# An mLSTM cell and a two-layer feed-forward on one core: the first product from chunk 1 on as three float32r products of 12-bit halves

## The chip, the cores and the metric

The kernel runs on one core of a Trainium2 chip. The metric is the device time of one execution in microseconds (us), the median of several runs. Engines are called TensorE (PE; its weight loads are PEld), VectorE (DVE), ScalarE (ACT), GpSimd (POOL) and SyncE (SP, which here only issues DMAs). SBUF is the on-chip memory with 128 partitions, PSUM holds the sums of TensorE in eight banks of 512 fp32 columns.

## The reference

Four batches, eight heads, 768 steps, head dimension 40. A recurrent attention (mLSTM) gives for each step a row of 320 = 8 x 40 values; the 3072 rows go through a feed-forward with a gelu of sigmoid form.

```python
for t in range(S):
    m_new = np.maximum(f_gate[:, :, t] + m, i_gate[:, :, t])
    f_stab = np.exp(f_gate[:, :, t] + m - m_new)
    i_stab = np.exp(i_gate[:, :, t] - m_new)
    C = f_stab * C + i_stab * outer(vt, kt)
    n = f_stab * n + i_stab * kt
    y[:, :, t] = sigmoid(o_gate) * (C @ qt) / np.maximum(abs(n @ qt), 1.0)
x = y as (3072, 320)
h = x @ w_in                                   # (3072, 2048)
g = h * (1.0 / (1.0 + np.exp(-1.702 * h)))
out = g @ w_out                                # (3072, 320)
```

All inputs are fp32 in value; the host hands them over as float64 bit pairs for `w_in` and `w_out`, which the kernel converts (lines 240 to 266).

## The kernel before

**Chunks.** The 768 steps are cut into six chunks w = 0 to 5 of 128 steps; a chunk has 4 x 128 = 512 tokens. The order of all work is written out by hand (`manual_schedule`): the loop over w at the end of the kernel issues, for each chunk, its first product `up`, then its second product `down`, and between the blocks of `down(w)` the attention of chunk w+1. Engines run their own instructions in the order in which they are issued, so a VectorE operation written behind another waits for it.

**First product.** `w_in` is held as 16 tiles of 128 output columns, two of its 320 rows' parts in `w_in_sb` (128 rows each) and the last 64 rows in `w_in_x`. Two tiles make a pair j, eight pairs make a chunk. Chunk 0 uses plain fp32 products (`up`, L626, L635). From chunk 1 on `up_fast` uses a scheme with seven products instead of eight for a 2 x 2 block product (Strassen's, in Winograd's form): half the tokens (256 columns) by sums of weight blocks. The weight sums are made once, in `input_sums` (L668 to L671, between blocks 11 and 13 of `down(0)`); the token sums in `token_sums` (L679 to L684) at the start of each chunk. Each pair is seven fp32 products of 256 columns (L724) and the products of the last 64 rows over 512 columns, two side by side on half the array's rows (L703). VectorE, ACT and POOL put the results together (L741, L763 to L765, L777, L778, L784, L786), and ACT applies gelu (L692) into `gs`.

**Second product.** `down_fast` is again a seven-product scheme, over two halves c of seven blocks each, so blocks 0 to 13 (L847, sums on VectorE L850, L852, L832). The blocks read `gs` and `sums`; block 10 is the last that reads the first four tiles of `gs`, block 11 the last that reads the first kind of `sums`, block 13 the last that reads the second. `store(1)` stands behind block 12 and `store(0)` behind block 13 (L856). `down(0)` is a plain product of 16 blocks (L793).

**Attention of the next chunk.** After each block the call list `attention(w + 1)` adds steps: gate columns (L367), weights (ACT L435, POOL L439), state products (`carry`, L602, L611, with `decay`, L579, and `scale`, L588), scores (L459, L462), values (L503, L511, L517 and on), then `seam_out` and `seam_in`, which send the result through DRAM, and `seam_turn` (VectorE, L572), which writes it transposed as `xT`, the input of the next first product. In the list the two halves of `seam_turn` stand behind blocks 10 and 11 (for chunk 1 behind blocks 12 and 14).

**Queues.** Nearly all DMAs are issued by SP in the written order. Ahead of block 13 SP issues `load_squares(w + 2)` (k and q of the chunk after next, L108), which `block_transposes` (L394) read during the next first product. During the first product SP issues the gate rows (`m_row`, `st_row`, `d_row`, L304 to L331), the o_gate load, the gate columns (`columns_in`, L350, L352), `spread` (L403) and the v and k loads (L120) of chunk w+1.

**Buffers.** Tiles with the same tag share buffers in turn: `gp` has eight of 4 KB per partition (`gs`), `sp` has four (`sums`), a new tile waits until the old one in its buffer is last read. `ps_m` is four PSUM banks, `ps_a` two pairs of banks.

Of the kernel before, what the change touches and what calls it, by code (L numbers as in the profile page):

```python
# [8 lines left out]
FP = mybir.dt.float32  # L9
U32 = mybir.dt.uint32  # L10
BF = mybir.dt.bfloat16
AF = mybir.ActivationFunctionType
OP = mybir.AluOpType
# [5 lines left out]
NEG = -1.0e30  # L19

# [6 lines left out]
def kernel(  # L27
# [33 lines left out]
    work = ctx.enter_context(tc.tile_pool(name="work", bufs=2))  # L61
    gp = ctx.enter_context(tc.tile_pool(name="gp", bufs=NH))
# [16 lines left out]
    s_in = const.tile([128, 3, NF // 2, 128], FP, name="s_in")  # L79
# [5 lines left out]
    w_in_sb = const.tile([128, 2, DFF], FP, name="w_in_sb")  # L85
    w_in_x = const.tile([128, NF // 2, 128], FP, name="w_in_x")
# [46 lines left out]
    def piece_in(c, n):  # L133
        return (w_in_sb[:, c, n * 512:(n + 1) * 512],
                [(slice(0, 128), slice(0, 512), w_in_bits[c:256:2, n * 1024:(n + 1) * 1024])])
# [21 lines left out]
    def fetch(n):  # L157
        if n < 3 or 10 <= n < 13:
            bits[n] = s_in[:, n % 10].rearrange("p j m -> p (j m)").bitcast(U32).rearrange("p (a two) -> p a two", two=2)
        elif n == 17:  # L160
            bits[n] = t_flat[:, at_bits:at_bits + 1024].bitcast(U32).rearrange("p (a two) -> p a two", two=2)
        else:
            bits[n] = (gp if 6 <= n < 10 else sp).tile([128, 512, 2], U32, tag="g", name="bits")
# [34 lines left out]
    ident = const.tile([128, 128], FP, name="ident")  # L198
# [155 lines left out]
    def columns_turn(w):  # L354
        c = cols[w] = gate.tile([L, 4 * BH], FP, name="cols")
# [3 lines left out]
    def columns(w):  # L359
        if w == 0:  # L360
            pt = banks("p_cols")[:, 0, :]
            T.transpose(pt[:, 0:3 * BH], stacked[w], full)
            c = cols[w] = gate.tile([L, 4 * BH], FP, name="cols")
# [157 lines left out]
    def x_of(w):  # L521
        if w not in xT:
            xT[w] = work.tile([128, 3, B, L], FP, tag="xT", bufs=1, name="xT")
        return xT[w]
# [43 lines left out]
    def seam_turn(w, c):  # L568
        for b in range(2):
            x = x_of(w)[:, :, 2 * c + b, :].rearrange("p c (r n) -> p n c r", n=4)  # L570
# [43 lines left out]
    def up(w, j, between):  # L614
# [5 lines left out]
        def full(j, first, cs=range(2)):  # L620
            for c in cs:
                for i in range(2):
                    f = 2 * j + i
                    for n in range(2):
                        t = slice(n * W // 2, (n + 1) * W // 2)
                        T.matmul(ph[j][i][:, t], w_in_sb[:, c, f * 128:(f + 1) * 128], x[:, c, t],  # L626
# [34 lines left out]
    half_w = W // 2  # L661
    temps, second = {}, {}

    def input_sums(js):

        a = lambda c, i: w_in_sb[:, c, :].rearrange("p (j two m) -> p j two m", two=2, m=128)[:, js, i, :]
        s1, s2, s4 = (s_in[:, n, js] for n in range(3))
        V.tensor_tensor(out=s1, in0=a(0, 1), in1=a(1, 1), op=OP.add)  # L668
        V.tensor_tensor(out=s2, in0=s1, in1=a(0, 0), op=OP.subtract)
        V.tensor_tensor(out=a(0, 1), in0=a(0, 0), in1=a(0, 1), op=OP.subtract)  # L670
        V.tensor_tensor(out=s4, in0=a(1, 0), in1=s2, op=OP.subtract)  # L671

    def token_sums(w):

        x = xT[w].rearrange("p c b t -> p c (b t)")
        b11, b12, b21, b22 = (x[:, c, n * half_w:(n + 1) * half_w] for c in range(2) for n in range(2))
        r = [work.tile([L, PH, D1], FP, tag="u", name="t_x").rearrange("p h d -> p (h d)") for _ in range(2)]
        x1, x2, x4 = r[0][:, 0:half_w], r[0][:, half_w:W], r[1][:, 0:half_w]
        V.tensor_tensor(out=x1, in0=b12, in1=b11, op=OP.subtract)  # L679
        V.tensor_tensor(out=x2, in0=b22, in1=x1, op=OP.subtract)  # L680
        V.tensor_tensor(out=b12, in0=b22, in1=b12, op=OP.subtract)
        V.tensor_tensor(out=x4, in0=b21, in1=x2, op=OP.subtract)
        rest = x[64:128, 2, :]
        V.tensor_tensor(out=rest[:, 0:half_w], in0=rest[:, 0:half_w], in1=rest[:, half_w:W], op=OP.subtract)  # L684
        temps[w] = {1: b11, 2: b21, 3: b22, 4: x4, 5: x1, 6: x2, 7: b12}
        second[w] = r[1][:, half_w:W]

    def gelu_fast(w, j, between=None):
        for i in (1, 0):
            if between and i == 0:  # L690
                between()
            A.activation(out=gs[w, j][:, i, :], in_=gs[w, j][:, i, :], func=AF.Gelu_apprx_sigmoid)  # L692

    row_banks = {}

    def row_product(w, j, start):

        n = 2 if w == NW - 2 or (w == NW - 3 and j < 2) else 1
        for h in range(n):
            t = slice(h * W // n, (h + 1) * W // n)  # L700
            for i, row in enumerate(row_banks[w, j]):
                r = slice(i * 64, i * 64 + 64)
                T.matmul(row[:, t], w_in_x[r, j, :], xT[w][r, 2].rearrange("p b t -> p (b t)")[:, t],  # L703
                         start=(start and h == 0), stop=(not start and h == n - 1))
# [4 lines left out]
    def up_fast(w, j):  # L709

        x = temps[w]
        k = j % 4
        left, right = slice(0, half_w), slice(half_w, W)
        f = lambda c, i: w_in_sb[:, c, (2 * j + i) * 128:(2 * j + i + 1) * 128]

        def product(n, out, start, stop):
            a = {1: lambda: f(0, 0), 2: lambda: f(1, 0), 3: lambda: s_in[:, 2, j], 4: lambda: f(1, 1),
# [16 lines left out]
        def copy_row():  # L739
            if apart:  # L740
                A.copy(out=g[:, 0, :], in_=row0)  # L741
# [296 lines left out]
```

## Time and profile before

| what | value |
|---|---|
| runs | 465.27 us median of three (463.86 to 467.92) |
| the profiled execution | 464.2 us, which is its span from the first to the last instruction |
| first product of chunks 1 to 5 | 112.65 to 144.50, 184.85 to 216.69, 256.09 to 287.94, 327.34 to 359.22, 398.46 to 430.30 us |
| granted TensorE clock | 1.000 of full speed in the mean |
| DMA | 52.87 MB, mean 114 GB/s over the span |

In the lines of the profile a group names the line of the kernel, the engine, the operation and output<-inputs, then the count, and after the bar the busy time and the mean of one. In the chain of work and in the timelines the columns are start, length and what, in us from the start of the span; a `q` behind an engine's name is its sequencer, which issues a DMA. An fp32 matmul shows as two instructions, each with its weight load.

### The profile page before, as it was taken

The numbers are of one execution on the slowest core, as the hardware profiler recorded it, in microseconds if no ns is written. First come the engines' busy times: TensorE is split into PE (matmuls) and PEld (weight loads), VectorE is DVE, ScalarE is ACT, GpSimd is POOL, SyncE is SP. The second block draws the span as 40 slices with busy tenths as digits, with TensorE's granted clock in tenths as the row PEclk, the third lists the DMA queues.
The fourth block names the chain that finished last, engine by engine and source line by source line (L and its number), as shares of the span: only waits on it lengthen the run. The fifth ranks groups of instructions, "written<-read, shape, count | busy, mean of one in ns | idle before, by whom it ended". The sixth has DMA issues, their size and how long they took to land.

```text
span 464.2 us, 12386 instructions
## 1 busy us (share of the span) xinstructions
PE 456.3 (98%) x5071; PEld 391.0 (84%) x5071; DVE 353.3 (76%) x738; ACT 186.4 (40%) x433; POOL 163.7 (35%) x154
## 2 busy tenths in 40 slices
PE   8999999899999999999999999999999999999996
PEld 6877887577779899779999779999888999787996
DVE  5788997989889975888786888787788766554622
ACT  5686779100556600455800354900264910164200
POOL 5101507200599600266800167610157710146200
PEclk9999999999999999999999999999999999999999
DMA  8999999018969025969224979315988505000000
GB/s 162 184 275 198 210 262 232 14 33 198 190 133 135 3 61 125 200 99 174 35 58 105 195 122 167 46 33 126 172 128 155 79 18 140 28 1 1 1 28 30
DMA packets 135561, 52.87 MB, mean 114 GB/s; under 512 B 101984, under 2 KB 131632, under 8 KB 135504
## 3 DMA queue, kind: packets, MB, share of 16 engines
q1 hardware_dynamic: 127136, 50.27, 55.6%
q10 hardware_dynamic: 8048, 1.66, 1.8%
q8 instruction: 40, 0.66, 0.7%
q0 software_dynamic: 320, 0.15, 0.2%
q14 instruction: 17, 0.14, 0.1%
HBM read 44.52 MB, written 7.54 MB: 112 GB/s over the span
## 4 chain that ended last, share of the span: by engine, by line
PE 79%; DMA 8%; DVE 7%; SPq 4%; issue 2%; ACT 0%; DVEq 0%
PE p_out L847 31%; PE p_h L724 22%; PE p_h L703 7%; PE p_out L793 3%; PE p_h L626 3%; PE p_o L503 2%; DMA q_sq<-in_q_dram 2%; PE p_i L511 2%; SPq L120 2%; PE p_c L602 2%; DMA st_row<-f_run 2%; PE p_s L459 2%; DMA t_sb<-in_moe_w_out_dram 2%; DMA bits<-in_moe_w_out_dram 1%; DVE state L579 1%
## 5 line engine op out<-in xcount | busy, mean ns | idle before, releaser
L784 POOL TENSOR_TENSOR g<-g,parts 128x512 f32<-128x512 f32 x30 | 38.2, 1274 | 196.8 <-ACT g L741 188.0
L763 ACT COPY parts<-p_h 128x256 f32<-128x256 f32 x40 | 14.9, 372 | 166.0 <-PE p_h L724 160.8
L847 PE MATMUL p_out<-w_out_sb,g 128*128 128x160 f32 x480 | 68.9, 300 | 0.0
L847 PEld LDWEIGHTS p_out<-w_out_sb,g 128*128 128x128 f32 x480 | 66.4, 190 | 0.5
L724 PE MATMUL p_h<-xT,w_in_sb 128*128 128x256 f32 x240 | 65.9, 383 | 0.0
L692 ACT ACTIVATE g<-g 128x512 f32<-128x512 f32 x80 | 47.8, 629 | 25.2 <-DVE g L778 18.8
L724 PEld LDWEIGHTS p_h<-xT,w_in_sb 128*128 128x128 f32 x240 | 44.6, 190 | 11.9 <-issue 5.5
L852 DVE TENSOR_TENSOR o_sb<-o_sb,p_out 128x160 f32<-128x160 f32 x70 | 21.3, 318 | 43.3 <-PE p_out L847 42.8
L847 PE MATMUL p_out<-t_sb,s 128*128 128x160 f32 x320 | 47.1, 300 | 0.0
L847 PEld LDWEIGHTS p_out<-t_sb,s 128*128 128x128 f32 x320 | 44.4, 190 | 0.2
L724 PE MATMUL p_h<-t_x,s_in 128*128 128x256 f32 x160 | 41.1, 379 | 0.0
L435 ACT ACTIVATE wt<-wt,cols 128x64 f32<-128x64 f32 x160 | 38.8, 334 | 0.1
L703 PE MATMUL p_h<-xT,w_in_x 64*128 64x512 f32 (+1 forms) x200 | 37.1, 514 | 0.0
L793 PE MATMUL p_out<-w_out_sb,g 128*128 128x320 f32 x128 | 35.7, 436 | 0.0
L724 PEld LDWEIGHTS p_h<-t_x,s_in 128*128 128x128 f32 x160 | 30.4, 190 | 4.1
L793 PEld LDWEIGHTS p_out<-w_out_sb,g 128*128 128x128 f32 x128 | 23.9, 190 | 9.6
L703 PEld LDWEIGHTS p_h<-xT,w_in_x 64*128 64x128 f32 x200 | 18.5, 186 | 14.9 <-issue 14.2
L741 ACT COPY g<-p_h 128x512 f32<-128x512 f32 x30 | 17.5, 583 | 32.0 <-PE p_h L703 17.8
L764 DVE TENSOR_TENSOR t_x<-p_h,parts 128x256 f32<-128x256 f32 x40 | 17.0, 425 | 16.8 <-ACT g L692 8.7
L626 PE MATMUL p_h<-xT,w_in_sb 128*128 128x256 f32 x128 | 29.6, 384 | 0.0
L778 DVE TENSOR_TENSOR g<-p_h,parts 128x512 f32<-128x512 f32 x40 | 27.7, 692 | 1.4
L626 PEld LDWEIGHTS p_h<-xT,w_in_sb 128*128 128x128 f32 x128 | 23.6, 190 | 5.3 <-issue 2.4
(205 smaller groups left out, 861.1 us busy)
## 6 DMA issues: line engine op xcount, KB each, us to landing
q_sq<-in_q_dram SPq DMA_DIRECT2D x20, 320.0 KB, 10.0
wt<-m_row SPq DMA_DIRECT2D x20, 256.0 KB, 5.4
k_sq<-in_k_dram SPq DMA_DIRECT2D x16, 320.0 KB, 6.4
out_dram<-o_sb SPq DMA_DIRECT2D x24, 160.0 KB, 1.9
eo<-in_o_gate_dram SPq DMA_DIRECT2D x5, 640.0 KB, 8.0
bits<-in_moe_w_in_dram SPq DMA_DIRECT2D x6, 512.0 KB, 11.6
q_sq<-x_row SPq DMA_DIRECT2D x10, 256.0 KB, 3.0
v_st<-in_v_dram SPq DMA_DIRECT2D x14, 160.0 KB, 5.9
```

What stands on the lines that cost most here:

```text
L435: A.activation(out=x[:, h, :], in_=x[:, h, :], func=AF.Exp, scale=-1.0, bias=cols[w][:, c * PH + h:c * PH + h + 1])
L626: T.matmul(ph[j][i][:, t], w_in_sb[:, c, f * 128:(f + 1) * 128], x[:, c, t], start=(first and c == 0 and n == 0), stop=(not first and c == ...
L692: A.activation(out=gs[w, j][:, i, :], in_=gs[w, j][:, i, :], func=AF.Gelu_apprx_sigmoid)
L703: T.matmul(row[:, t], w_in_x[r, j, :], xT[w][r, 2].rearrange("p b t -> p (b t)")[:, t], start=(start and h == 0), stop=(not start and h == ...
L724: T.matmul(out, a, x[n], start=start, stop=stop)
L741: A.copy(out=g[:, 0, :], in_=row0)
L764: V.tensor_tensor(out=u2, in0=p56[:, right], in1=y[:, left], op=OP.add)
L778: V.tensor_tensor(out=g[:, 1, :], in0=row1, in1=y[:, half_w:3 * half_w], op=OP.add)
L784: G.tensor_tensor(out=g0, in0=g0, in1=u, op=OP.add)
L793: T.matmul(po, gs[w, f // 2][:, f % 2, b * L:(b + 1) * L], w_out_sb[:, f, :], start=(f == 0), stop=(f == NF - 1))
L847: T.matmul(po, a(f), b[:, f, :], start=(f == 0), stop=(f == NH - 1))
L852: V.tensor_tensor(out=dst, in0=x, in1=po, op=OP.add)
```

## The change

From chunk 1 on the first product has no block sums. Each fp32 operand is split into a high and a low part, each stored as float32r (an fp32 word whose low bits are dropped on writing; the halves have 12 bits). With B = 2^12, the product of x and w is put together from three products: high x high, low x low and difference x difference, where the difference is formed of an operand and its high part. Each is one matmul over all 512 tokens.

- **Weights**: `split_in(n)`, n = 0 to 3 (512 columns each), behind blocks 7, 9, 11 and 13 of `down(0)`: ACT writes `w_high`, VectorE `w_diff`, POOL `w_low`; SP stores all four `w_diff` and `w_low` of n = 1, 2 in DRAM. `split_rest` behind block 10 stacks high and low of the last 64 rows in one 128-row tile. `w_high`, and `w_low` of n = 0, 3, stay in SBUF. The other `w_low` (buffers of `gs`) and all `w_diff` (buffers of `sums`) are fetched anew for each chunk from 2 on: `fetch_low` behind block 10, `fetch_diff` of n = 0, 1 behind block 11, of n = 2, 3 behind block 13.
- **Tokens**: `split_x` behind each half of `seam_turn`: two ACT copies of 512 and 256 columns, five VectorE operations of 256.
- **Products**: per pair, two PSUM banks `main` (high and low, two row parts each) and two `side` (differences, two row parts, then the last 64 rows with their high and low stacked); even pairs use `ps_m`, odd ones `ps_a`. ACT copies `side` with a scale, VectorE adds `main`, one gelu covers both tiles.
- **Moved**: the o_gate load of the next chunk from pair 0 to the end of the first product; the k and q transposes one pair later; `open_gates` of chunks 2 on from behind block 1 to behind block 2. `token_sums`, `input_sums`, POOL's additions (L784) and the row products go.

```diff
-    w_in_sb = const.tile([128, 2, DFF], FP, name="w_in_sb")
-    w_in_x = const.tile([128, NF // 2, 128], FP, name="w_in_x")
+    w_in = [win.tile([128, 2, 512], FP, tag="wa", name="w_in") for _ in range(3)]
+    w_in.append(t_flat[:, at_bits:at_bits + 1024].rearrange("p (c m) -> p c m", c=2))
+    w_in_x = work.tile([128, NF // 2, 128], FP, tag="xh", bufs=1, name="w_in_x")
...
+    def rooms(w):
+        for c in range(2):
+            xT[w, c] = gp.tile([128, 3, 2, L], FP, tag="g", name="xT")
+        for n in range(4):
+            if n not in low_kept:
+                w_low[w, n] = gp.tile([128, 2, 512], FR, tag="g", name="w_low")
+        for n in (0, 2, 1, 3):
+            w_diff[w, n] = sp.tile([128, 2, 512], FR, tag="g", name="w_diff")
+    def split_in(n):
...
+        A.activation(out=w_high[n], in_=src, func=AF.Copy, scale=BIAS)
+        V.scalar_tensor_tensor(out=w_diff[1, n], in0=w_high[n], scalar=-1.0 - 1.0 / BASE, in1=src, op0=OP.mult,
+                               op1=OP.add)
+        G.tensor_tensor(out=low, in0=src, in1=w_high[n], op=OP.subtract)
...
+                nc.sync.dma_start(out=row[n], in_=x.rearrange("p c m -> p (c m)").bitcast(FP))
+    def split_rest():
...
+        for i, r in ((0, slice(0, 64)), (1, slice(64, 128))):
+            A.activation(out=wr[r, i::2], in_=w_in_x[r], func=AF.Copy, scale=BIAS)
+        A.copy(out=wr[0:64, 1::2], in_=wr[64:128, 1::2])
+        G.tensor_tensor(out=wr[64:128, 0::2], in0=w_in_x[0:64], in1=wr[0:64, 0::2], op=OP.subtract)
+        G.tensor_tensor(out=wr[64:128, 1::2], in0=w_in_x[64:128], in1=wr[64:128, 1::2], op=OP.subtract)
+    def split_x(w, c):
...
+        A.activation(out=high, in_=x[:, 0:2], func=AF.Copy, scale=BIAS)
+        A.activation(out=rest_high, in_=x[:, 2], func=AF.Copy, scale=-BIAS / BASE)
+        for k in range(2):
+            V.scalar_tensor_tensor(out=x_diff[w][k][:, t], in0=high[:, k], scalar=-1.0 - 1.0 / BASE, in1=x[:, k],
+                                   op0=OP.mult, op1=OP.add)
+        for k in range(2):
+            V.scalar_tensor_tensor(out=low[:, k], in0=x_diff[w][k][:, t], scalar=BASE, in1=high[:, k], op0=OP.mult,
+                                   op1=OP.add)
+        V.scalar_tensor_tensor(out=rest_low, in0=x[:, 2], scalar=-1.0 / BASE, in1=rest_high, op0=OP.mult,
+                               op1=OP.subtract)
...
     def up_fast(w, j):
+        mains = [(lambda i, k=k: w_high[n][:, k, col(i)], x_high[w][:, k]) for k in range(2)]
+        mains += [(lambda i, k=k: low[:, k, col(i)], x_low[w][:, k]) for k in range(2)]
+        sides = [(lambda i, k=k: w_diff[w, n][:, k, col(i)], x_diff[w][k]) for k in range(2)]
+        sides += [(lambda i: w_rest[0][:, 2 * j + i], x) for x in x_rest[w]]
...
+        passes(main, mains)
+        passes(side, sides)
...
+        for i in range(2):
+            A.activation(out=g[:, i, :], in_=side[i], func=AF.Copy, scale=-BASE)
+        for i in range(2):
+            V.scalar_tensor_tensor(out=g[:, i, :], in0=main[i], scalar=1.0 + 1.0 / BASE, in1=g[:, i, :], op0=OP.mult,
+                                   op1=OP.add)
...
-        at = (0, 1, 3, 3, 5, 6, 8, 8, 9, 12, 14) if w == 1 else (0, 0, 1, 3, 1, 4, 5, 6, 6, 10, 11)
+        at = (0, 1, 3, 3, 5, 6, 8, 8, 9, 12, 14) if w == 1 else (0, 0, 1, 3, 2, 4, 5, 6, 6, 10, 11)
...
-                    load(w + 1, "o")
...
-                    for n in ((0, 2), (), (4,), (6, 1, 3), (5, 7), (), ())[j - 1]:
+                    for n in ((), (0,), (2, 4), (6, 1), (3, 5), (7,), ())[j - 1]:
...
             gelu_fast(w, NF // 2 - 1)
+            if more:
+                load(w + 1, "o")
             hidden_sums(w, (2, 3), V)
...
-            if w == 0 and i in (11, 13):
-                input_sums(slice(0, 4) if i == 11 else slice(4, 8))
+            if w == 0 and i in (7, 9, 11, 13):
+                split_in((i - 7) // 2)
+            if w == 0 and i == 10:
+                split_rest()
+            if w and more:
+                if i == 10:
+                    fetch_low(w + 1)
+                if i == 11 or i == 13:
+                    fetch_diff(w + 1, (0, 1) if i == 11 else (2, 3))
```

## The prediction, on record before the changed kernel ran

> **What bounds the kernel now.** I read the page first, then the chain of work in order of time, then one stretch between two chunks on each queue. The page says that TensorE hardly ever rests:
>
> ```profile
> span 464.2 us, 12386 instructions
> ...
> PE 456.3 (98%) x5071; PEld 391.0 (84%) x5071; DVE 353.3 (76%) x738; ACT 186.4 (40%) x433; POOL 163.7 (35%) x154
> ```
>
> The chain (start, length, what) shows one period: the second product of chunk 2 (L847), the first product of chunk 3 (L724, L703), the next second product. Nothing stands between them, so what TensorE saves is saved, and any new wait of TensorE costs its full length. The first two lines are from the kernel's start: bf16 matmuls of 512 columns.
>
> ```profile
> 10.54 0.22 PE p_w L429
> 10.76 0.22 PE p_w L427 x4
> ...
> 240.68 15.41 PE p_out L847 x112
> 256.09 3.02 PE p_h L724 x14
> 259.11 3.64 PE p_h L703 x24
> 262.76 12.28 PE p_h L724 x56
> 275.04 3.63 PE p_h L703 x16
> 278.67 9.26 PE p_h L724 x42
> 287.94 8.69 PE p_out L847 x64
> 296.63 2.01 PE p_c L602 x128
> ```
>
> A first product takes 287.94 - 256.09 = 31.85 us; the other four agree to 0.04. The timeline of VectorE just before it starts (block 10 of the second product ends at 249.4, blocks 11 to 13 take 2.17 each), and one line from the first chunk:
>
> ```profile
> 81.78 3.20 DVE L579 TENSOR_TENSOR state<-state_mid,cols 128x328 f32<-128x328 f32 x1
> ...
> 249.85 1.56 DVE L572 STREAM_TRANSPOSE xT<-q_sq 128x256 f32<-128x256 f32 x4
> 251.25 0.73 DVE L832 TENSOR_TENSOR s<-g,s 128x256 f32<-128x256 f32 x2
> 251.91 0.54 DVE L852 TENSOR_TENSOR o_sb<-o_sb,p_out 128x160 f32<-128x160 f32 x2
> 252.37 1.61 DVE L572 STREAM_TRANSPOSE xT<-q_sq 128x256 f32<-128x256 f32 x4
> 253.96 0.32 DVE L852 TENSOR_TENSOR o_sb<-o_sb,p_out 128x160 f32<-128x160 f32 x1
> ```
>
> The input of chunk 3 is ready at 254.0, 2 us before TensorE wants it. SP's queue at the same place, and the DMA view of that stretch (size, median us to landing):
>
> ```profile
> 254.30 0.36 SPq L856 DMA_DIRECT2D out_dram<-o_sb  x1
> 254.71 2.08 SPq L108 DMA_DIRECT2D k_sq<-in_k_dram  x4
> 256.89 5.39 SPq L108 DMA_DIRECT2D q_sq<-in_q_dram  x4
> ```
>
> ```profile
> q_sq<-in_q_dram SPq DMA_DIRECT2D x4, 320.0 KB, 11.2
> ...
> st_row<-f_run SPq DMA_DIRECT2D x1, 48.0 KB, 8.1
> ```
>
> 48 KB take 8.1 us only because they stand behind the q loads: this queue serves in order. The last q load is issued at 260.6 and lands about 11 later, 271.6, so the eight loads fill 254.71 to 271.6 = 16.9 us. Two rows of the view by stretches give the rate (last column, GB/s) for large and for these small packets:
>
> ```profile
> 44.00:48.00 4.00, 4.00 (x46) 3.36 (x45) 3.61 (x7) 2.97 (x7) 0.00 (x0) 1.00 1.07 353
> ...
> 255.00:259.00 4.00, 4.00 (x23) 3.33 (x21) 2.74 (x8) 0.37 (x1) 0.00 (x0) 1.00 0.94 197
> ```
>
> **The change, part by part.**
>
> *TensorE.* 56 products of 256 columns and 16 row products of 512 become, per chunk, 16 tiles x 8 float32r products of 512 columns = 128. Their price is in no row. An fp32 matmul is two instructions; L724 gives 12.28/56 = 0.219 for two passes of 256 columns, so four passes of 512 take 0.877. Lower end: one pass, 0.219 (the bf16 row, 0.22; faster is excluded, as no row streams 512 columns in less). Upper end: half an fp32 matmul, 0.44. I take 0.219, since an operand of one 12-bit half leaves one product of the four. Then 128 x 0.219 = 28.07 (3.51 per pair j of tiles), 3.78 less than 31.85, over five chunks -18.9. The weight load before each matmul I cost at nothing: L724 has as many loads as matmuls and they lie beside the matmuls. [...]
>
> *Evacuation.* Per pair, ACT copies two 512-wide banks (0.583 each, L741) and does one gelu (twice 0.63, L692): 2.4. VectorE has two PSUM operations (0.69 each, L778). Both lie under 3.51 of TensorE; with two bank sets a pair has 3.5 us for it. Only the gate work (4.1 us, 118.0 to 122.1) after pair 0 breaks this: pair 1 is emptied at 7.55 after pair 0's end, pair 3 starts at 7.0: 0.5 us. POOL loses six additions of 1.27.
>
> *The start of chunks 2 to 5.* Moved ahead of the last blocks' work, VectorE gets per half five operations of 256 columns (0.42 each; 0.40 apart, from L679 to L684) and two waits for ACT's copy (0.44 each, from 0.6 for 512 columns). From 249.6: addition 0.24, turn 1.40, wait 0.44, split 2.0, L832 0.66, L852 0.46, turn 1.40: ACT starts at 256.4 and ends at 257.0. TensorE waits 1.0 for it, 0.3 for the low half, and 0.4 for the banks of blocks 12 and 13, whose additions now queue behind the second split (ending 259.0 to 259.5): 1.8 (bounds 1.0 and 2.5). The token sums that go were beside TensorE.
>
> *The differences of tiles 8 to 15, chunks 2 to 4.* Behind block 12's addition SP waits with its store, and behind that store stand the k and q loads, the last store, and the second pair of difference fetches, whose buffers are the sums that block 13 reads. So: store 259.3, k loads from 259.6 instead of 254.7, q landed at 259.6 + 16.9 = 276.5, then 0.5 MB at 350 GB/s = 1.5: landed at 278.3 with 0.3 of latency. Pair 4 wants it at 256.1 + 4 x 3.51 + 1.75 = 271.9. TensorE loses 6.4 (the 1.8 included), and the product ends at 278.3 + 1.75 + 3 x 3.51 = 290.6, 2.6 later than now. Lower end: VectorE without its ACT waits, 1.0 later; upper 3.5. The low halves and the first two differences (2 MB, 6 us from 251.1 on an idle queue) land by 258, needed at 259.4: nothing; if the stretch's 197 GB/s held, 3.4. SP's issues of these six fetches (0.43 in L167's median) stand before nothing that is due.
>
> *After that*, st_row lands behind the differences at about 282, column loads are issued by 284.5, and spread, v and k follow. Now they take 278.4 to 295 = 16.5; then k is in at 301, wanted by the state product 8.7 after 290.6 = 299.3. Without the o_gate load (moved behind them, wanted 12.8 after the end) they may be 2 faster: 0 to 4, I take 1.2. So chunks 2, 3 and 4 cost 3 x (2.6 + 1.2) = +11.4. Chunk 5 has no loads in the way: 1.8 - 3.78 = -2.0.
>
> *The start of chunk 1.* VectorE is full from 104.5 to 114.2 already. Out go eight sums of 0.68 and part of five of 0.42; in come three splits of 1024 columns (1.1 each, by 0.85 per column from L473 and L478), waiting for ACT's 1.05 each (L374) behind its DMA issues (to 105.6), and both halves' splits. In order: 103.6 second attention half, 107.9 split 1, 112.1 split 2, 113.5 turn, 116.1 split of x, 117.6 split 3, 119.0 turn, 119.6 ACT; TensorE stands ready at 112.6: 7.0, and 0.5 for banks. This has no contention with POOL, which gets five operations of 2.35 (L806: 2.9 for 1280) just there. L579 above took 3.20 instead of 0.50 while L806 ran from 81.7 to 84.6. If VectorE waits out a POOL operation nearly each time it starts a group (three of 2.35), 14. I take 10.5, midway: both engines are released by the same ACT copies, but no row says which comes first. [...] L806 of 81.7 now comes after the splits, so L579's wait (TensorE lost 1.8 behind it) may go, but a split on POOL stands there: 0 to -1.8, I take -0.9. The six stores of 0.5 MB delay the next k loads to about 119, wanted at 134. Chunk 1: -3.8 + 10.5 + 0.5 - 0.9 = +6.3.
>
> Sum: 6.3 + 11.4 - 2.0 = +15.7 on 464.2, 479.9. The median of the runs is 465.27, 1.1 above the profiled execution: 481.
>
> **Rivals.** *The differences come in time* (not slower). If the fetches are not served behind k and q, pair 4 has its tile by 273.7 (271.9 + 1.8) and k comes early too: chunks 2 to 4 give -2.0 each instead of +3.8, sum -1.7, 463.6 us; with 7.5 for chunk 1's start, 460.6. For it: 352 GB/s are possible, and the queue is idle from 252.8 to 254.7. Against it: the 8.1 us of st_row. Its range is 456 to 468.
> *Float32r costs two passes*: 128 x 0.44 = 56.3, +24.4 per chunk. The differences are then wanted at 256.1 + 31.7 = 287.8, so their wait is gone: 122 + 4 x 1.8 + 9.6 = +139, 604 us. For it only that no row shows float32r.
> *ACT becomes the bound* would need 3.5 per pair; its rows make 2.4: not counted.
>
> **How the numbers follow.** My forecast 0.62, its own range 468 (7.5 at chunk 1, -1.8, 1.0 per chunk, k in time) to 495 (14; 3.5 and 3 per chunk); in time 0.27; two passes 0.11. About 1% is what a measurement of this kernel can tell from no change: 460.6 to 469.9. Faster: 0.15, of the second case. Same: 0.12 of it and 0.05 of mine. Slower: 0.57 + 0.11. The range 459 to 498 leaves out the two passes and about 0.08 of the second case.
>
> **What would show it.** Float32r matmuls 0.22 apart (0.44: the second rival). In chunks 2 to 4, TensorE waiting in pair 4 for a w_diff DMA, 4 to 7 us; a start wait on ACT or VectorE of 1 to 2.5; in chunk 1, one of 7 to 14. VectorE's 1024-column splits at 1.1 free and up to 3.4 beside POOL. If w_diff lands before pair 4 wants it, or if TensorE is slowed by evacuation, my account is wrong.

## The result and the profile after

The changed kernel takes 492.05 us (median of four runs, 489.22 to 494.02) against 464.56 of the kernel before beside it: ratio 1.059 with a 95% interval of 1.053 to 1.065. The forecast was 481, range 459 to 498, slower at 0.68. The profiled execution took 489.22, its span is 487.5. Medians here are over all executions of a kernel, while the ratios leave out the few that lie over 1.5% above its fastest (one in experiment 2, two of six in 9, one of twelve in 12; without them the medians are 485.6, 472.2 and 466.6). From the page after:

```profile
span 487.5 us, 12031 instructions
...
PE 451.5 (93%) x4951; PEld 390.3 (80%) x4951; DVE 338.4 (69%) x669; ACT 212.1 (44%) x430; POOL 143.3 (29%) x130
...
PEclk9999999996699999998999998999999999999999
...
DMA packets 139879, 68.57 MB, mean 141 GB/s; under 512 B 102464, under 2 KB 132112, under 8 KB 139824
```

TensorE is busy 93% instead of 98%, its clock dips where it was full (0.975 granted in the mean for 1.000), and 15.7 MB more are moved. What TensorE waited for (total, times, longest):

```profile
PE p_h L760 <- ACT x_high L726: 18.3, 5, 15.7
PE p_h L760 <- DMA w_diff<-w_row: 10.9, 3, 4.4
```

Both waits are the forecast ones, at the forecast places: the start of each first product (L760) and the differences of pair 4 in chunks 2 to 4. The first is mostly one wait of 15.7, chunk 1's. VectorE there:

```profile
107.68 2.77 DVE L689 SCALAR_TENSOR_TENSOR w_diff<-w_high,w_in 128x1024 fp32r<-128x1024 f32 x1 [2.56 <-ACT w_high L688]
110.37 1.53 DVE L578 STREAM_TRANSPOSE xT<-q_sq 128x256 f32<-128x256 f32 x4
113.36 4.49 DVE L729 SCALAR_TENSOR_TENSOR x_diff<-x_high,xT 128x256 fp32r<-128x256 f32 x2 [1.46 <-ACT x_high L726]
117.78 3.43 DVE L732 SCALAR_TENSOR_TENSOR x_low<-x_diff,x_high 128x256 fp32r<-128x256 f32 x2
...
124.98 0.76 DVE L729 SCALAR_TENSOR_TENSOR x_diff<-x_high,xT 128x256 fp32r<-128x256 f32 x2 [0.47 <-ACT x_high L726]
```

The same pair of operations (L729) takes 4.49 us at 113 and 0.76 at 125. In between, GpSimd's work stops; its timeline:

```profile
103.54 3.40 POOL L691 TENSOR_TENSOR w_low<-w_in,w_high 128x1024 fp32r<-128x1024 f32 x1 [18.20 <-ACT w_high L688]
107.02 2.34 POOL L704 TENSOR_TENSOR w_rest<-w_in_x,w_rest 64x1024 fp32r<-64x1024 f32 x1
109.44 3.23 POOL L705 TENSOR_TENSOR w_rest<-w_in_x,w_rest 64x1024 fp32r<-64x1024 f32 x1
112.74 2.35 POOL L691 TENSOR_TENSOR w_low<-w_in,w_high 128x1024 fp32r<-128x1024 f32 x1
115.17 2.40 POOL L691 TENSOR_TENSOR w_low<-t_sb,w_high 128x1024 fp32r<-128x1024 f32 x1
117.53 3.05 POOL L791 TENSOR_TENSOR t_sb<-w_out_sb 128x1280 f32<-128x1280 f32 x1
```

Six operations without a break, 103.5 to 120.6. The last is a weight sum that stood at 81.7 before. One more wait: ScalarE's first copy of the tokens stood 5.05 us behind L705, since `x_high` takes the buffer of `w_in_x`, which L705 still reads.

SP's queue in chunk 2 shows the other stall in the order foreseen:

```profile
199.70 2.08 SPq L114 DMA_DIRECT2D k_sq<-in_k_dram  x4
201.82 5.32 SPq L114 DMA_DIRECT2D q_sq<-in_q_dram  x4
207.24 1.43 SPq L841 DMA_DIRECT2D out_dram<-o_sb  x1
208.76 1.30 SPq L714 DMA_DIRECT2D w_diff<-w_row  x2
```

Counted from where TensorE is free (196.66), k is issued at +3.0 (worked out: +3.5), the last q has landed at +20.7 (+20.4) and the difference that TensorE wants at +21.8 (+22.2). Then comes what no step of mine had. In these rows, one for each stretch, the next to last number is the share of the DMA engines and the one before it the granted clock:

```profile
216.00:219.00 3.00, 0.36 (x2) 0.35 (x3) 0.46 (x1) 0.00 (x0) 0.98 (x1) 1.00 0.70 236
219.00:221.00 2.00, 2.00 (x7) 1.58 (x6) 0.00 (x0) 0.00 (x0) 0.00 (x0) 0.56 0.02 4
221.00:223.00 2.00, 2.00 (x7) 1.59 (x6) 0.86 (x2) 1.09 (x2) 0.00 (x0) 0.59 0.10 16
```

After an idle of 4.39 us TensorE works for 3.41 us at half clock (0.5 granted from 219.22 to 222.64; the rows are means over their stretch). The last product of the chain, which has no wait, gives the price of float32r:

```profile
424.20 29.71 PE p_h L760 x128
```

29.71/128 = 0.232 us for 512 columns. With this as the clean length, the 23.3 us between the two profiled spans (487.5 - 464.2) divide so:

| term | forecast | measured |
|---|---|---|
| five products, 29.71 for 31.85 | -18.9 | -10.7 |
| idle before chunk 1 | +10.5 | +15.7 |
| half clock in chunk 1's product (32.04 long) | 0 | +2.3 |
| start waits, chunks 2 to 5 | +7.2 | +2.6 (four of 0.65) |
| difference waits, chunks 2 to 4 | +13.8 | +10.9 (4.39, 2.75, 3.79) |
| the rest of these three products: half clock in chunks 2 and 3, none in chunk 4 | 0 | +4.0 (1.84, 1.88, 0.25) |
| k_st and the rest of the second products | +3.6 | +1.8 (of it +2.7 in chunk 3) |
| end of chunk 0 | -0.9 | -3.3 |
| gate work in chunk 1 | +0.5 | 0 |

### The profile page after: what moved, and what is told of

It is laid out like the page before. It is cut to its first block, busy times and chain, and to the rows that moved or that the text cites. A ratio compares the mean times of both kernels' runs of the same rounds, so it can differ in the third digit from the quotient of the medians.

```text
span 487.5 us, 12031 instructions
## 1 busy us (share of the span) xinstructions
PE 451.5 (93%) x4951; PEld 390.3 (80%) x4951; DVE 338.4 (69%) x669; ACT 212.1 (44%) x430; POOL 143.3 (29%) x130
## 2 busy tenths in 40 slices
DMA packets 139879, 68.57 MB, mean 141 GB/s; under 512 B 102464, under 2 KB 132112, under 8 KB 139824
## 5 line engine op out<-in xcount | busy, mean ns | idle before, releaser
L770 DVE SCALAR_TENSOR_TENSOR g<-p_h,g 128x512 f32<-128x512 f32 x80 | 51.5, 684 | 65.8 <-ACT g L768 65.5
L768 ACT ACTIVATE g<-p_h 128x512 f32<-128x512 f32 x80 | 43.4, 594 | 52.4 <-PE p_h L760 52.3
L760 PE MATMUL p_h<-x_high,w_high 128*128 128x512 f32 x160 | 45.7, 409 | 18.3 <-ACT x_high L726 18.3
L738 ACT ACTIVATE g<-g 128x1024 f32<-128x1024 f32 x40 | 42.4, 1061 | 35.8 <-DVE g L770 35.7
L760 PE MATMUL p_h<-x_diff,w_diff 128*128 128x512 f32 x160 | 44.4, 400 | 10.9 <-DMA w_diff<-w_row 10.9
L760 PEld LDWEIGHTS p_h<-x_high,w_high 128*128 128x128 f32 x160 | 31.2, 198 | 26.9 <-ACT x_high L726 19.8
L760 PEld LDWEIGHTS p_h<-x_diff,w_diff 128*128 128x128 f32 x160 | 30.3, 192 | 18.7 <-issue 9.0
L760 PE MATMUL p_h<-x_rest,w_rest 128*128 128x512 f32 x160 | 45.1, 405 | 0.0
L760 PE MATMUL p_h<-x_low,w_low 128*128 128x512 f32 x160 | 44.3, 399 | 0.0
L760 PEld LDWEIGHTS p_h<-x_low,w_low 128*128 128x128 f32 x160 | 30.6, 193 | 7.8 <-DVE x_low L732 1.5
L760 PEld LDWEIGHTS p_h<-x_rest,w_rest 128*128 128x128 f32 x160 | 31.1, 195 | 6.8
```

The source lines that it names most:

```text
L738: A.activation(out=gs[w, j], in_=gs[w, j], func=AF.Gelu_apprx_sigmoid)
L760: T.matmul(dst[i], a(i), x, start=(m == 0), stop=(m == len(what) - 1))
L768: A.activation(out=g[:, i, :], in_=side[i], func=AF.Copy, scale=-BASE)
L770: V.scalar_tensor_tensor(out=g[:, i, :], in0=main[i], scalar=1.0 + 1.0 / BASE, in1=g[:, i, :], op0=OP.mult, op1=OP.add)
```

## The experiments

The theory: at the start of chunk 1 VectorE and ScalarE stand behind GpSimd's part of the weight split; in chunks 2 to 4 the differences stand in one line of transfers; each long idle costs half clock on top. The ratios are to the kernel before on the same chip (medians 463.6 to 465.1), with their 95% intervals. All but 7 and 8 start from the changed kernel.

### 1. The second pair of differences fetched ahead of k and q

```diff
-            if w + 2 < NW and i == 13:
-                load_squares(w + 2, "kq" if w else "k")
...
                     fetch_diff(w + 1, (0, 1) if i == 11 else (2, 3))
+                if i == 13 and w + 2 < NW:
+                    load_squares(w + 2, "kq")
```

> The k and q loads of the chunk after next are issued behind the second pair of difference fetches instead of ahead of them; nothing else changes. Queue order (my theory): in the changed kernel w_diff 2 landed 1.2 us behind the last q load; now it lands some 3 us after block 13, the waits of TensorE in pair 4 (4.4, 2.8, 3.8 us) and the half clock that followed two of them (1.7 each) go: about -14 us, 478. k and q land 3 to 4 us later; if VectorE's transposes then hold up the emptying of banks, 2 to 3 us per chunk come back (486). Rival, the fetch itself is slow or its buffer comes free late: the waits stay within 1 us of what they were, 491.

496.19 us, ratio 1.068 (1.062 to 1.074). The w_diff waits are gone, the products of chunks 2 to 5 take 29.7 each, and nothing is gained:

```profile
PE p_h L760 <- ACT x_high L726: 18.0, 5, 15.4
PE p_c L608 <- DMA k_st<-in_k_dram: 10.2, 2, 5.1
PE p_c L608 <- POOL state_mid L585: 3.6, 1, 3.6
```

What stands behind the transfers in the line is now late: 13.8 us of waits at the state product for the 10.9, with half clock after them. The waits of the differences do come from the order of one queue, as the theory says, but my 478 was wrong, and the 486 with it: behind the place to which k and q were moved, other transfers were needed just as soon.

### 2. GpSimd's part held back until chunk 1's tokens are split

```diff
-            if w == 0 and i in (7, 9, 11, 13):
-                split_in((i - 7) // 2)
+            if w == 0 and i == 7:
+                split_in(0)
+            if w == 0 and i in (9, 11):
+                high_in((i - 7) // 2)
+                diff_in((i - 7) // 2)
...
+                if w == 1 and j == 0:
+                    wait_for(x_rest[1][1][:, 256:512])
+                    low_in(1)
+                    low_in(2)
+                    split_in(3)
+                    weight_sums(0)
```

> POOL's low halves of weight columns 512 to 2047, the whole split of the last 512 columns and the weight sums of the second product are held until the tokens of chunk 1 are split, so that POOL does only the two operations for the last 64 rows beside VectorE's splits. Contention (my theory): VectorE's pairs of x splits fall from 4.5 and 3.4 us to 0.8, chunk 1 starts at 117 instead of 125, its clock drops less: -8 to -10 us, 482. Rival, the start is set by the order of ACT and VectorE and by the buffer that x_high shares with w_in_x: the start moves by less than 2.5, time 489 to 492.

485.89 us, ratio 1.044 (1.039 to 1.049): 6.2 less than the changed kernel. The idle falls from 15.7 to 7.1. `high_in`, `diff_in` and `low_in` are the three parts of `split_in`; the last quarter's split on ScalarE and VectorE (`split_in(3)`) is held back with GpSimd's part. GpSimd now has nothing to do from 109.6 to 118.6, and VectorE's operations have their free lengths:

```profile
112.65 0.76 DVE L739 SCALAR_TENSOR_TENSOR x_diff<-x_high,xT 128x256 fp32r<-128x256 f32 x2 [0.53 <-ACT x_high L736]
113.33 0.75 DVE L742 SCALAR_TENSOR_TENSOR x_low<-x_diff,x_high 128x256 fp32r<-128x256 f32 x2
```

The contention is shown: the same line 4.49 us beside GpSimd, 0.76 without it, and with the next line (3.43 and 0.75) that makes 6.4 of the 8.6 us. The profiled spans differ by 3.6 only (483.9 for 487.5): chunk 1's product is 0.8 longer by a gap behind VectorE and has its half clock as before, and after the difference waits there is more half clock, 6.83 us for 3.41 in chunk 2 and 3.41 for none in chunk 4.

### 3. ScalarE's work and the remaining differences spread as well

```diff
             if w == 0 and i == 7:
                 split_in(0)
+                high_in(1)
+                split_rest()
+                high_in(2)
+            if w == 0 and i == 9:
+                diff_in(1)
+                diff_in(2)
+                wait_for(ys[1, 1][:, 1, :])
+                low_rest()
```

> As the second kernel of these runs (the lows, the last split and the weight sums held back until chunk 1's tokens are split), and besides ScalarE's highs of the weights and of the rest columns are made at once after block 7, the differences after block 9, and GpSimd's rest lows only after the last values. Nothing is left out. My theory (the idle before chunk 1's product is VectorE and ScalarE queued behind or slowed by the weights' split): that idle falls from 15.7 us (7.1 in the second kernel) to about 3, the chunk 1 product starts near 112.5 and runs at full clock in about 30; total about 479, 475 to 482. Rival (what is left of the 7.1 is the token path itself, transposes and loads of the square): the idle stays at 6 to 7 and the total at 485 to 487. Rival (the work put together early slows the second product of chunk 0): the start is early, but TensorE comes to the seam later by as much.

483.34 us, ratio 1.039 (1.033 to 1.044). The idle is 2.72, as expected. The total lies above the expected 475 to 482: the product of chunk 1 still takes 32.4 for 30 (half clock and a gap of 0.79 behind VectorE), and behind the difference waits, which stay at 10.9, chunks 2 and 4 have more half clock than in the change (products of 36.9 and 35.2 for 35.9 and 33.8).

### 4. Dummy matmuls in the wait

```diff
             if w == 1:
                 weight_sums(0)
+                keep_busy(68, banks("p_idle")[:, 0, :])
```

> 68 bf16 matmuls of zeros (0.216 us each, 14.7 us) fill TensorE's wait before chunk 1; they write a bank that nobody reads. Clock theory: the first product of chunk 1 took 32.0 us against 29.7 in chunk 5 because the granted clock was 0.5 for its first 6 us; with the clock kept at 1.0 it takes 29.5 and the time falls by 2.4, to 489.5. Rival, chunk 1 is slow for another reason (gate work, POOL): no change, 492.

495.77 us, ratio 1.068 (1.062 to 1.073). The clock theory holds in its stage: no half clock, chunk 1's product takes 29.77 for 32.04. Yet the total is 3.7 us above the changed kernel instead of 2.4 below it. The second product behind it, untouched, takes 42.5 for 39.6, with idles of 0.49, 1.10 and 0.68 that the profile puts down to "issue", as in chunk 3 of the changed kernel. I had no cause for these yet; 6 and 7 give it.

### 5. One instruction for 256 columns instead of 512

```diff
-                    T.matmul(dst[i], a(i), x, start=(m == 0), stop=(m == len(what) - 1))
+                    for h in range(2):
+                        t = slice(h * W // 2, (h + 1) * W // 2)
+                        T.matmul(dst[i][:, t], a(i), x[:, t], start=(m == 0 and h == 0),
+                                 stop=(m == len(what) - 1 and h == 1))
```

> Each float32r product of 512 columns is made as two of 256 with the same weights, each with its own weight load. In the changed kernel the products start 0.227 us apart, where a bf16 or half an fp32 product of as many column passes takes 0.216 to 0.219. If the 0.227 is a rate per column (0.44 ns), two halves take 0.227 as well and a first product 29.7; if it is 14 ns per instruction over 0.213, halves start 0.121 apart and a first product grows by 1.9 us to 31.6; if the weight load bounds, they start 0.13 to 0.19 apart and it grows by 4 to 19 us.

494.86 us in one execution. Chunk 5's product takes 31.88 for 256 instructions, 0.1245 each, against 0.232 for 512 columns. The difference is 0.1075 per 256 columns, so 0.215 for 512 and some 0.017 fixed per instruction: one pass, with a small cost that the fp32 row (0.219 for two passes of 256) did not contain.

### 6. k loaded early, q behind the differences

```diff
-            if w + 2 < NW and i == 13:
-                load_squares(w + 2, "kq" if w else "k")
+            if w + 2 < NW and i == (4 if w else 13):
+                load_squares(w + 2, "k")
...
                     fetch_diff(w + 1, (0, 1) if i == 11 else (2, 3))
+                if i == 13 and w + 2 < NW:
+                    load_squares(w + 2, "q")
```

> Order of loads only: in chunks 1 to 3 the loads of k for the next turn are issued at block 4 of the second product, when the DMA queue stands nearly idle, instead of at block 13, and those of q behind the last difference fetch. 320 KB (6 to 8 us of the queue) leave the line in front of the differences. Theory (the line of transfers at the seam is what the fetched differences, or with them put first the v and k_st loads, wait for): no wait for w_diff and none over 1 us at the state product; the products of chunks 2 to 4 take 29.7 each, total 478, 475 to 481. Rival (v_st and k_st are late for another reason than the line's length, their own issue waits): the state product waits 3 to 5 us in three chunks as with the fetches first, total 490 to 496.

486.35 us, ratio 1.047 (1.042 to 1.053). The line theory is confirmed for the waits it speaks of: none for w_diff or k_st, products of 29.7 to 30.0 in chunks 2 to 5, which is some 14 us back. But the total is above the expected 475 to 481, since 7 are lost again:

```profile
PE p_h L760 <- ACT x_high L726: 18.3, 5, 15.5
PE p_s L465 <- issue: 7.2, 3, 3.1
```

In the timeline of TensorE the scores break off in the middle, with no semaphore to wait for:

```profile
169.21 1.39 PE L465 MATMUL p_s<-qT,kT 40*64 40x64 f32 x72
173.66 1.56 PE L465 MATMUL p_s<-qT,kT 40*64 40x64 f32 x48 [3.06 <-issue]
```

The queues of the page say what is late:

```profile
q8 instruction: 39, 0.64, 0.6%
```

There are 39 packets of 16,384 bytes for the 9980 instructions of TensorE in the trace (2 x 4951 matmuls and weight loads and 78 others), and 44 for the 11,278 of experiment 5: one for 256 instructions in both. So this queue carries TensorE's program. In the trace the packet due here starts at 170.98, after the idle has begun (170.60) and as the third of the four k loads, 320 KB each, lands (170.74); it takes 1.38 us, and TensorE goes on at 173.66. In the other two stretches such a packet lies inside or just ahead of the idle too (245.1 and 319.3), and so it was in 4, where packets end 0.3 to 0.9 us before each of the three idles.

### 7. The same move in the kernel before

```diff
-            if w + 2 < NW and i == 13:
-                load_squares(w + 2, "kq" if w else "k")
+            if w + 2 < NW and i == (4 if w else 13):
+                load_squares(w + 2, "k")
+            if w and w + 2 < NW and i == 13:
+                load_squares(w + 2, "q")
```

> The kernel before, with its loads of k for the next turn issued at block 4 of the second product of chunks 1 to 3 instead of at block 13 (q stays at 13); its float32r product, split and fetches do not exist. Theory (idles of TensorE that the profile puts down to issue are instruction packets, 16 KB each on a queue of their own, that come late behind the k loads' packets): idles of 1 to 3 us before the score matmuls in two or three chunks, each with such a packet starting late inside or just ahead of it, and a total 3 to 8 us longer, 467 to 472, though a load is merely moved to an idle stretch of the queue. Rival (those idles belong to the changed kernel alone, its wait or its clock): no new idle, within 1 us of the kernel before.

467.57 us, ratio 1.004 (1.000 to 1.007). The idles are there in the kernel that has no float32r, no split and no fetch, the first with its packet starting 0.15 us before it (156.02, 1.40 long), between the landing of the third k load (155.96) and the fourth (157.36):

```profile
155.13 1.03 PE L459 MATMUL p_s<-qT,kT 40*64 40x64 f32 x52
158.79 1.58 PE L459 MATMUL p_s<-qT,kT 40*64 40x64 f32 x76 [2.62 <-issue]
```

Three idles, 3.6 us, and half clock after the first. The total moves by less than the expected 3 to 8 us, and by the time alone it could not be told from no change; the trace carries it.

Counting TensorE's instructions in all traces shows where it stopped. Of 34 idles over 0.3 us that the profiles put down to issue, in twelve kernels, 33 begin at the same place of a block of 256: behind instruction 193 plus a multiple of 256, among them 3265, 5057 and 6849 both here and in 6, though the kernels differ in their matmuls. In each of the 33 TensorE went on 1.23 to 1.56 us after one of the packets had ended. So in these it stopped at the end of a block because the next one had come late. (The one that does not fit is of 0.47 us, in 12.)

The run also corrects a term of mine: chunk 0, where nothing was edited, ends at 110.11 here, and at 112.65 in the profile of before. There VectorE's transposes (L394) waited for the last q load, which landed 2.2 us later than here (77.26 for 75.10), and the state update behind them (L579) then started at 81.78, beside GpSimd's L806 (81.72), and took 3.20. Here it was done before L806 began (at 81.35). One line of before, then one of this run:

```profile
77.34 4.01 DVE L394 STREAM_TRANSPOSE qT<-q_sq 128x512 f32<-128x512 f32 x4 [2.55 <-DMA q_sq<-in_q_dram]
```

```profile
79.62 0.64 DVE L579 TENSOR_TENSOR state<-state_mid,cols 128x328 f32<-128x328 f32 x1
```

### 8. The first weight sum moved in the kernel before

```diff
+                wait_for(xT[1][:, 1, 3, :])
                 weight_sums(0)
```

> The kernel before with one edit: the first weight sum on GpSimd waits until chunk 1's tokens have been turned, as it in effect does after the change; nothing else is touched. In the kernel before that sum stands beside the last copies out of PSUM of chunk 0's second product, which took 3.20 us for one that takes 0.92 after the change. Theory (that contention is the 3.2 us that the changed kernel has ahead at the end of chunk 0): 462, faster by 2 to 3.2 us. Rival (the end of chunk 0 is early, but the token sums then wait for the same turn): within 0.7 us of the kernel before.

467.51 us, ratio 1.006 (1.003 to 1.008): slower, as neither theory had it. Chunk 0 ends at 110.21, but the weight sum now meets the token sums, where L680 takes 3.14 (0.42 otherwise); TensorE waits 2.5 us for it and has 3.4 us of half clock. The state update had started at 79.62 here too, so this run does not show what the edit does to chunk 0. By 7 and 8, some 2.5 of the 3.3 us of chunk 0 are not the change's own: they come from the late q load in the profiled execution of before.

### 9. Spread split and k early together

The edits of 3 and 6.

> The split spread out (first kernel of this call) and k loaded early (third) together: both waits gone at once. If the two are independent, the gains add: about 492 less 13 less 14, some 465, 462 to 469, which is the kernel before within a per cent. Rival (one stall takes the other's place, as the fetches first did): 472 or more.

473.95 us, ratio 1.016 (1.012 to 1.021). 18 us less than the changed kernel, but above the expected 469, in the rival's range: in the profiled execution, which took 477.64, the issue idles remain (5.8 us before the scores, 1.0 before the values).

### 10. k behind the values

As 9, with:

```diff
-            if w + 2 < NW and i == (4 if w else 13):
+            if w + 2 < NW and i == (6 if w else 13):
                 load_squares(w + 2, "k")
```

> The split spread out as before, and k loaded early, but at block 6 of the second product, behind the store that waits for block 5, instead of at block 4: the loads then run beside the last small matmuls and not beside the scores and the first values. Theory (late instruction packets took 7 of the 14 us that the early load gave back): the score idles of 1 to 3 us go, the products of chunks 2 to 4 stay at 29.7 to 30, total 465 to 469. Rival (the idles are not from the loads): they stay, and the total with them at 473 to 474. Rival (the k packets now hold up the token transfers behind them): the start waits of chunks 2 to 4 grow from 0.66 to 2 or more, total 471 to 478.

473.83 us, ratio 1.020 (1.016 to 1.024), above the expected 465 to 469 and no better than 9. The large score idles go (0.8 in all), but one of 4.88 comes in the value product of chunk 3, again with k on the queue (issued 306.9 to 308.8, landed 311.5 to 316.3) and a packet that starts at 315.06, behind the third load. In chunks 1 and 2 a packet starts as the third load lands too (171.7 and 242.6), but there TensorE reaches the end of its block only 1.5 us or more after the packet has ended, and there is no such idle. The start waits grow to 1.0 and 1.3 in chunks 2 and 3. The place of this idle is given by the blocks (it begins at instruction 7361, as the 0.49 of the changed kernel does); the length differs with the loads (4.88 for 0.49).

### 11. A warm start

As 10, with:

```diff
+            if w == 1:
+                keep_busy(12, banks("p_idle")[:, 0, :])
             for j in range(NF // 2):
                 up_fast(w, j)
```

> The kernel of the run before with 12 bf16 matmuls on the idle tile in front of chunk 1's product (their result is not used), in the 2.7 us in which TensorE waits there. Theory (the idle costs half clock afterwards): no half clock in chunk 1's product, 29.7 to 30.5 instead of 31.4 to 32.4, total 1.5 to 2 us less than the run before. Rival (a 2.7 us idle at that place does not lower the clock by itself, or the dummy work delays the start): the same within 1 us.

469.44 us, ratio 1.012 (1.008 to 1.015). No half clock in chunk 1, product 31.4 with one gap of 1.34 behind VectorE. That the dummy matmuls did this is not shown: in the profiled execution of 9, without them, the idle of 2.70 at this place had no half clock after it either, while those of 2.72 (3) and 2.69 (10) had it. The median is 4.4 less than in 10, more than the 2 expected, but the two profiled spans are almost the same (470.8 and 471.0), so these traces do not show where it comes from.

### 12. In chunk 3 no early load

As 11, with:

```diff
-            if w + 2 < NW and i == (6 if w else 13):
+            if w + 2 < NW and w < 3 and i == (6 if w else 13):
                 load_squares(w + 2, "k")
...
-                if i == 13 and w + 2 < NW:
-                    load_squares(w + 2, "q")
+                if w + 2 < NW and i == (11 if w == 3 else 13):
+                    load_squares(w + 2, "kq" if w == 3 else "q")
```

> As the run with the split spread, k behind block 6 and the warm start, but in chunk 3 alone (where the idles of 3.2 and 4.9 us before the value matmuls were) k is not loaded early: there k and q go behind the first pair of difference fetches, at block 11, ahead of the seam's last stores. Theory (those idles are instruction packets behind the k loads' packets): no idle over 1.1 us in the second product of chunk 3 and no half clock there, 3 to 6 us less; against it the second pair of differences of chunk 4 is again fetched behind k and q, a wait of 0 to 3.8 us and up to 1.7 for half clock. Total 464 to 468. Rival (the idle belongs to the place, not to the loads): it stays, total 469 or more.

466.85 us, ratio 1.006 (1.003 to 1.008). No idle above 0.5 us in chunk 3's second product, none of its half clock, and one difference wait; an issue idle of 1.4 stays in chunk 1's second product:

```profile
span 465.3 us, 12054 instructions
...
PE 450.2 (97%) x4963; PEld 388.2 (83%) x4963; DVE 335.5 (72%) x669; ACT 211.7 (45%) x430; POOL 144.8 (31%) x132
...
PEclk9999999989999999999999999999999999999999
```

```profile
PE p_h L773 <- ACT x_high L739: 3.3, 4, 1.3
...
PE p_out L845 <- issue: 1.4, 1, 1.4
PE p_h L773 <- DVE g L783: 1.3, 1, 1.3
...
PE p_h L773 <- DMA w_diff<-w_row: 1.0, 1, 1.0
```

Some 25 of the 27.5 us are back with the order of work and the 12 dummy matmuls alone; the arithmetic, the split and the traffic (68.57 MB) are those of the change. It does not beat the kernel before. Against the profile of before, the five products save 7.9 us (151.4 for 159.3), and the start of chunk 1 (+2.9), the stretches between products 1 to 5 (+2.4, +2.1, +0.8, +1.2) and the end (-0.4) spend 9.0.

## Why the prediction was right, and where it was off

The forecast, slower and inside the range, came out by the two stalls it named: the idle before chunk 1 and the difference waits make +26.6 us against the -10.7 of the products. The table has the parts. Of the ranges that I had listed as signs, the distance of the float32r products (0.23 for 0.22) and the lengths of VectorE's weight splits (1.21 free, 2.77 beside GpSimd) came out; chunk 1's wait (15.7 for 7 to 14), the start waits (0.65 for 1 to 2.5) and two of the three difference waits (2.75 and 3.79 for 4 to 7) did not.

- **TensorE.** One pass is right, two passes (604) refuted. The price was mis-sized: 0.232 for 0.219, 8.2 us over five chunks. Experiment 5 puts the difference into the instruction, not the columns. The load beside each matmul cost little here: of the 0.232, 5 gives 0.215 to the columns, which leaves an estimated 0.017 for the load and everything else that an instruction costs.
- **The start of chunk 1.** That VectorE is held up beside GpSimd is shown by 2 (0.76 for 4.49 with GpSimd idle); the size was 15.7 for 10.5. Failed in it: "midway" between 7.0 and 14, GpSimd's work taken as five operations where six ran without a break, and ScalarE's 5.05 us behind the buffer of `w_in_x`, which I had not traced. The 14, in which VectorE waits out a GpSimd operation nearly each time, was the nearer end: beside GpSimd its operations took 4.49 for 0.76 and 2.77 for 1.21.
- **Half clock.** No term of mine had it; 6 us in three products. Experiment 4 takes it away in chunk 1 by keeping TensorE busy (granted 1.00 from 125 to 155; 0.91 from 125 to 157 in the change).
- **Start waits of chunks 2 to 5.** 0.65 for 1.8. The splits are as long as assumed (0.76, 0.75 and 0.41 for 2.0) and the wait for ScalarE's copy is 0.65 for 1.0; the 0.3 for the low half and the 0.4 for the banks did not come.
- **Differences.** Right in cause and place (1, 6), 10.9 for 13.8. The wanted one landed 1.1 behind the last q for 1.8; the 0.3 of latency in the 1.8 was an estimate that no run shows by itself.
- **After that.** k_st did not come late (0 of 3.6) as the change stands. It does so as soon as the differences are put first (1), so the reserve there is small.
- **Chunk 0.** -3.3 for -0.9; by 7 and 8 mostly the late q load in the profiled execution of before.

The parts that were too high and too low partly cancel: 9.3 us too much loss in the waits of chunks 2 to 5 (24.6 for 15.3, half clock apart), 2.4 too little gain in chunk 0 and the 0.5 of the gate work stand against 8.2, 5.2 and 6.3 (0.3 of it without half clock). With the terms that were too low alone corrected the sum would have been 501, outside the range; that the result lies inside it is in part luck. The rival that the differences come in time did not happen in the change. 12 comes near it, with the start repaired too, and is no gain either: my 463.6 left out the 8.2 us by which the float32r products were priced too low.

Left open: the idles of chunk 3 in the changed kernel itself (0.81, 0.52, 0.49) stand at the ends of blocks, each with an instruction packet that ended less than a microsecond before (starts at 321.4, 326.4 and 331.4). But little data is moved then (0.05 of the DMA engines' time from 320 to 334), so why these packets come late was not settled. Nor is it settled why four runs of the change have a median 2.8 us above its profiled execution.

## What to carry to other kernels

When a kernel is full of hand-placed loads, a stage cannot be priced by its own waits: moving one transfer moved the stall to the next in line (1), then to TensorE's own program (6), and only with each transfer in a slot that was free for data and for instructions was nearly all the time back (12). Where VectorE is to run beside GpSimd, count every GpSimd operation that stands in the way, buffers included, and take the held-up length when the trace shows it once (3.20 in before for the 0.64 of 7, 4.49 in the change for the 0.76 of 2). And add to an idle of TensorE the half clock that may follow it (here 2.3, 1.84 and 1.88 us behind 15.7, 4.39 and 2.75, and none behind 3.79).

## What the runs showed of the hardware

- **The program came by DMA and could be late.** 16 KB packets on a queue of their own, one for 256 instructions of TensorE (39 for 9980 in the change, 40 for 10,233 before), mostly 0.9 to 1.5 us long; in 33 of the 34 idles counted in 7 TensorE stopped at the end of a block and went on 1.23 to 1.56 us after a packet had ended. Beside four k loads of 320 KB it stood up to 4.9 us (10). Small matmuls used a packet's worth in about 4 us (packets start at 231.3, 235.4, 239.6 and 243.4 in the trace of before). In 6 the idles came to 7.2 us.
- **Half clock after an idle was not decided by its length alone.** It followed idles of 1.44 (3), 1.54 (12), 2.48 (8), 2.62 (7), 2.75 and 4.39 (the change), and not those of 1.45 (before), 2.70 (9) and 3.79 (the change, chunk 4), while 3.74 at that last place had it (2). In the change it was granted for 3.41 us twice (from 219.22 and from 294.32) and for 17.07 once (from 113.41 to 130.48, of which TensorE stood until 125.00).
- **One load that came late put two engines side by side.** With the last q load landing 2.2 us later, VectorE's L579 ran beside GpSimd's L806 and took 3.20 us for 0.64, and chunk 0 ended 2.5 us later (before and 7, one execution each).
